# Four layers on one core: the first pair's layer norm in the last spectral round spread over every second product, its roots made together, and the first projections one product later

## The chip, the core and the metric

The program runs on one core of a Trainium2 chip as a single launch. The metric is the device time of one execution in microseconds (us); three executions of the kernel before gave a median of 2034.66 us (2031.99 to 2038.42). A core has a matrix engine (PE), a vector engine (DVE), an activation engine (ACT), a general engine (POOL) and a queue for transfers (SP). Each runs its instructions in the order in which they stand in its own queue; an instruction that waits for another engine holds up all that stand behind it.

## The reference

The input x has 2048 rows of 640 values. Four layers follow each other, each with a norm ahead and a residual sum behind: spectral, attention, spectral, attention.

```
def layernorm(x): return (x - mean(x)) / sqrt(var(x) + 1e-5)          # over the 640 columns

def spectral(x):                       # real part of a two-dimensional Fourier transform
    a, b = x @ Wd_re.T, x @ Wd_im.T
    return Ws_re @ a - Ws_im @ b

def attention(x):                      # 32 heads of 20, each query sees 256 keys back
    q, k, v = split(x @ wqkv)
    return softmax(mask(q @ k.T * 20 ** -0.5)) @ v @ wo

x = x + spectral(layernorm(x));  x = x + attention(layernorm(x))      # twice over
```

## The kernel before

Rows go in 16 tiles of 128. A number in f32 that enters a matrix product is split in two halves of 16 bits, a high one (rounded by ACT) and a low one (the rest, made by DVE or POOL), and a product is made of three: high by high, high by low, low by high.

**A spectral layer** has four rounds (`r`), each over four tiles of the transformed input, and in each round eight steps (`j`), each for two tiles of 128 output rows. A step makes seven products of twelve matmuls (128x320). `main_a` makes one (`x`), `main_c` then closes the step before with two (`z`, `y`), `main_b` makes four (`y`, `x`, `z`, `y`); so a row of products reads x z y | y x z y. The letters are banks of the matrix memory (PSUM). Three products of a step start a bank and are later added to in place: the second half of such a pair may not begin until the add that reads the first half is done (DVE, `add`, L583, written `res<-z`, `res<-y`, `pf<-y`). After the last round the sums are the next layer's input, written to DRAM (`x2d`).

Beside its products a step prepares the seven factors of the step after. A block of the matrix comes by DMA (`cq`, 1 MB), POOL makes four sums of its quarters (`cs`, L549 to L552), ACT makes seven high halves (`cc`, L557), DVE seven low halves (`cc`, L560). Input blocks, sums, and later the stacked keys share three large buffers, so one is filled when the last reader of what was there is done.

**What sets the order.** Behind each product stands a call of `tick()`. It lets out the next split (one low half and the next high half) and takes one step of every generator in the list `side`; a generator's `yield` thus means "go on after the next product". A scheduler then sets each engine's own order from this; it keeps dependencies and such marks as `issue_after`, and can let an instruction pass others of its engine. The order rows in the prediction are what stands in each queue in the end.

**The last round** (`r == NR - 1`) prepares the attention as well. When step 0 is closed, its two output tiles are the first pair of rows for the attention. `finish(j, pace)` (L655) loads them back, takes the steps of `norm_steps` with `pace` yields for each, then transposes the two normed tiles on PE (`transposed`, L449: a block of three and one of two 128x128 transposes for each tile, `pf<-idf,lny`; ACT copies the high half, L455, DVE takes the low one, L456). The side list holds `finish(0, 1)` for the first pair and behind it, in one chain, `finish(1, 1)` for the second. `ahead` (L643), put on the list at step 3, waits until the first pair is transposed, yields once, and then makes ten projection products of 15 matmuls each (`Projections.qk`, L370, 128x256), five for the keys and five for the queries of the first block, one per tick. ACT takes each out of PSUM (`qf`, L386), POOL splits it (L387, L388), SP stores it (`qkd<-early`). At the head of step 7 whatever `ahead` has left is run at once, and the stacks of keys and queries are loaded (`ks<-onesd`, `ks<-qkd`). Behind the last product `drain()` runs what the side list still holds, and the attention begins with a value projection (`pf<-big,early`, 15 matmuls 128x320, taken out by ACT L902) and scores (`sq<-ks`). Transposes, projections and value projections all take their PSUM bank from one ring of two (`new_f`).

**`norm_steps`** (L131) first takes two `bn_stats` halves and a `bn_aggr` for each tile (L138, L141; a yield after the first half and one after the sum), then the inverse root by bits and three Newton steps on columns of one value per row: for each tile L147, L148, three times L150 and L151, and with `act` L155; two yields per tile. With `act`, two more yields and then one ACT pass per tile (L163, `lny`). For a pair this is 4 + 4 + 2 + 2 = 12 yields. `finish` is the only caller with a pair and `act`.

The last round occurs twice, once in each spectral layer; its steps 3 to 7 lie at about 464 to 548 us and 1470 to 1554 us of the profile.

Of the kernel before, what the change touches and what calls it, by code (L numbers as in the profile page):

```python
# [13 lines left out]
I32 = mybir.dt.int32  # L14
AF = mybir.ActivationFunctionType
OP = mybir.AluOpType
# [38 lines left out]
ROOT = float(0x5F3759DF - (1 << 22) - (1 << 30))  # L55
# [9 lines left out]
X_UP = 2.0 ** 10  # L65
# [8 lines left out]
def body(ctx: ExitStack, tc: tile.TileContext, x_in, cmat, whid, wqkv, wo, out):  # L74
    nc = tc.nc
# [40 lines left out]
    normed = [None]  # L116
# [14 lines left out]
    def norm_steps(xs, ys, act=False):  # L131

        n = len(xs)
        mv = keep.tile([P, n, 2], F32, tag=f"lnmv{n}", name="lnmv", bufs=2)
        for k, x in enumerate(xs):
            st = keep.tile([P, 2, 6], F32, tag="lnst", name="lnst", bufs=2)
            for h in range(2):
                nc.vector.bn_stats(st[:, h], x[:, h * 320:(h + 1) * 320])  # L138
                if h == 0:
                    yield  # L140
            nc.vector.bn_aggr(mv[:, k], st.rearrange("p a b -> p (a b)"))  # L141
            yield
        t = keep.tile([P, 3, n], F32, tag=f"lnt{n}", name="lnt", bufs=2)
        ts = nc.vector.tensor_scalar
        for k in range(n):
            h, g, u = (t[:, m, k:k + 1] for m in range(3))
            ts(h, mv[:, k, 1:2], 1e-5, -0.5 * X_UP ** -2, op0=OP.add, op1=OP.mult)  # L147
            ts(g.bitcast(I32), h.bitcast(I32), -0.5, ROOT, op0=OP.mult, op1=OP.add)  # L148
            for m in range(3):
                ts(u, g, g, h, op0=OP.mult, op1=OP.mult)  # L150
                normed[0] = ts(g, u, 1.5, g, op0=OP.add, op1=OP.mult).ins  # L151
                if m == 0:
                    yield
            if act:
                normed[0] = ts(u, mv[:, k, 0:1], g, -1.0, op0=OP.mult, op1=OP.mult).ins  # L155
            yield
        for _ in range(2 if act else 0):
            yield
        for k, x in enumerate(xs):
            g, u = t[:, 1, k:k + 1], t[:, 2, k:k + 1]  # L160
            y = keep.tile([P, D], F32, tag="lny", name="lny", bufs=2)
            if act:
                nc.scalar.activation(y, x, AF.Identity, bias=u, scale=g)  # L163
            else:
                normed[0] = ts(y, x, mv[:, k, 0:1], g, op0=OP.subtract, op1=OP.mult).ins
            ys.append(y)
            yield

    def layer_norm(xs):
        ys = []  # L170
        for _ in norm_steps(xs, ys):
            pass
        return ys
# [7 lines left out]
    def load(out, in_):  # L181
        with ExitStack() as order:
            if in_turn[0] and loads:
                order.enter_context(tc.issue_after(loads[-1]))
            elif floor:
                order.enter_context(tc.issue_after(floor[-1]))
            i = nc.sync.dma_start(out, in_)
        loads.append(i.ins)
# [211 lines left out]
    def spectral(layer, res_src, hidden, first):  # L400
        with ExitStack() as st:
# [11 lines left out]
            splits, side, marks = [], [], {}  # L413
# [8 lines left out]
            def tick(cut=True):  # L422
                if splits and cut:
                    with behind():
                        for f in splits.pop(0):
                            f()
                with behind():
                    for g in list(side):
                        if next(g, None) is None:
                            side.remove(g)  # L430
# [18 lines left out]
            def transposed(y, k, xt):  # L449
                d0, d1 = ((0, 3), (3, ND))[k]  # L450
                pt = new_f()[:, :(d1 - d0) * P].rearrange("p (a b) -> p a b", a=d1 - d0)
                for dt in range(d0, d1):
                    transpose(pt[:, dt - d0], y[:, dt * P:(dt + 1) * P], idf)
                hi, lo = (xt[:, m, d0:d1] for m in range(2))
                nc.scalar.activation(hi, pt, AF.Copy)  # L455
                nc.vector.scalar_tensor_tensor(lo, pt, 1.0, hi, op0=OP.mult, op1=OP.subtract)  # L456
# [50 lines left out]
            def side_norm(s):  # L507
                x, ys = load_x(s), []
                for _ in range(3):
                    yield 1  # L510
                for _ in norm_steps([x], ys, True):
                    yield 1
                split_x(s, ys[0], nc.gpsimd)
                yield 1
# [55 lines left out]
            def product(r, bank, cc, m, start, stop):  # L570
                o = bank[:, :HD]
                n = 0
                for k in range(RS):
                    zc = hidden.zc[RS * r + k]
                    for a, b in ((0, 0), (0, 1), (1, 0)):
                        matmul(o, cc[m][:, a, k * P:(k + 1) * P], zc[:, m, b],
                                         start=start and n == 0, stop=stop and n == 3 * RS - 1,
                                         skip_group_check=True)
                        n += 1
                return o  # L580

            def add(o, z, f):
                marks["dve"] = nc.vector.scalar_tensor_tensor(o, z, Y_DOWN, f, op0=OP.mult, op1=OP.add).ins  # L583
# [44 lines left out]
            def main_c(r, j):  # L628
                res, cc, y, zb = state.pop((r, j))
                x0, x1 = res  # L630
                z = product(r, zb, cc, 6, False, True)
                add(x0[:, hi], z, x0[:, hi])
                tick()
                z = product(r, y, cc, 5, False, True)
                add(x1[:, lo], z, x1[:, lo])
                last = r == NR - 1
                for k in range(2):
                    load((x2_d if last else acc_d)[2 * j + k], res[k])
                if last and j == 0:
                    side.append(chain(finish(0, 1), finish(1, 1)))  # L640
                tick()

            def ahead(proj):  # L643
                while finished[0] < 2:
                    yield 1
                yield 1
                for w in (1, 0):
                    for ct in range(ND):
                        for _ in proj.qk(0, w, ct):
                            pass  # L650
                        yield 1
# [3 lines left out]
            def finish(j, pace):  # L655
                xs = [sb.tile([P, D], F32, tag="xin", name="x2", bufs=NXIN) for k in range(2)]
                for k in range(2):
                    load(xs[k], x2_d[2 * j + k])
                for _ in range(3):
                    yield 1  # L660
                ys = []
                for _ in norm_steps(xs, ys, True):
                    for _ in range(pace):
                        yield 1
                for _ in range(2):
                    yield 1
                proj.new_rows(j)
                for k, y in enumerate(ys):
                    for m in range(2):
                        transposed(y, m, proj.rows[j][0][:, k])  # L670
                        yield 1
                    finished[0] += 1
# [95 lines left out]
            for r in range(NR):  # L768
# [24 lines left out]
                for j in range(NJ):  # L793
                    n = r * NJ + j
# [5 lines left out]
                    if r == NR - 1 and j == 3:  # L800
                        early_qk = ahead(proj)
                        side.append(early_qk)
# [20 lines left out]
                    with ExitStack() as order:  # L823
                        if j == 0 and r == 0 and first:
                            order.enter_context(tc.issue_after(hidden.last))
                        main_a(r, j)
                        if j:
                            main_c(r, j - 1)
                        main_b(r, j)
                    if r < NR - 1 and j in STAGES[r]:  # L830
                        k = STAGES[r].index(j)
                        s = RS * (r + 1) + k
                        turned_x(s)
                        if k < RS - 1:
                            turn_x(s + 1, 2)
                        z_stage(s)
                main_c(r, NJ - 1)
                if r == NR - 1:
                    drain()
# [672 lines left out]
```

## Time and profile before

| | |
|---|---|
| three executions, median (range) | 2034.66 us (2031.99 to 2038.42) |
| the profiled execution | 2034.73 us |
| its span, first to last instruction | 2033.0 us |
| PE busy | 1978.8 us, 97% |
| DVE busy | 1556.2 us, 77% |
| POOL busy | 1438.2 us, 71% |
| ACT busy | 1098.1 us, 54% |
| mean granted PE clock | 0.999 |

The profile is of one execution. A row of a timeline reads: start and length in us, engine, line, operation, what it writes and reads, shapes, and a count where like instructions follow each other; in square brackets the time that the engine stood idle before it and what ended the wait. Lengths of matmuls overlap: a row's next start less its start is what it costs PE. Line numbers are those of the kernel before.

### The profile page before, as it was taken

What the parts mean: (1) busy time and instruction counts of PE and PEld (TensorE: products, weight loads), DVE (VectorE), ACT (ScalarE), POOL (GpSimd) and SP (SyncE); (2) the same over time, 40 slices, a digit from 0 to 9 for tenths busy, and PEclk for the clock granted to TensorE, in tenths of its full rate; (3) what the DMA queues carried; (4) which work ended last, traced back from release to release, by engine and by line L of the source; (5) the groups of instructions that cost most, each with busy time, mean ns of one, the idle gap of its engine ahead of it and who ended that gap; (6) DMA issues with size and microseconds to landing.
All of it is one profiled execution on the core that took longest, in us unless ns stands there. A gap on an engine that the chain in (4) does not pass through costs nothing.

```text
span 2033.0 us, 55567 instructions
## 1 busy us (share of the span) xinstructions
PE 1978.8 (97%) x21761; PEld 1446.6 (71%) x21761; DVE 1556.2 (77%) x3281; ACT 1098.1 (54%) x1962; POOL 1438.2 (71%) x2148
## 2 busy tenths in 40 slices
PE   7999999999999999999999999999999999999998
PEld 5777777776777777777667777777677677777765
DVE  8888788767688888777648778787766788886674
ACT  5444555543257677666644444444332577766665
POOL 4667788877568788765557778777774687777754
PEclk9999999999999999999999999999999999999999
DMA  8566467566545545434545465454754455443232
GB/s 276 185 195 212 167 212 233 184 240 213 144 99 130 126 112 122 101 100 114 157 133 179 157 183 183 150 171 150 266 184 122 106 124 123 118 120 94 75 81 80
DMA packets 280507, 311.08 MB, mean 153 GB/s; under 512 B 107572, under 2 KB 214836, under 8 KB 271156
## 3 DMA queue, kind: packets, MB, share of 16 engines
q1 hardware_dynamic: 279668, 306.88, 51.3%
q8 instruction: 170, 2.79, 0.6%
q14 instruction: 93, 0.76, 0.1%
q10 hardware_dynamic: 576, 0.66, 0.1%
HBM read 201.72 MB, written 83.46 MB: 140 GB/s over the span
## 4 chain that ended last, share of the span: by engine, by line
PE 72%; DVE 12%; issue 4%; ACT 3%; DMA 2%; POOL 2%; SPq 0%; DVEq 0%; ACTq 0%; POOLq 0%
PE pf L125 33%; PE y L125 12%; PE x L125 12%; PE z L125 8%; PE sk L125 5%; DVE cc L560 3%; PE sq L125 3%; DVE sq L1216 2%; ACT ptq L1272 2%; DVE m L1218 2%; DMA res<-accd 1%; DVE lnst L138 1%; DVE lnt L150 1%; DVE res L583 1%; DVE lnt L151 1%
## 5 line engine op out<-in xcount | busy, mean ns | idle before, releaser
L125 PEld LDWEIGHTS <-cc 128*128 128x128 f16 x5376 | 525.9, 98 | 211.2 <-issue 11.1
L1272 ACT ACTIVATE ptq<-sk,shift,alpha 128x768 f32<-128x768 f32 (+2 forms) x512 | 472.7, 945 | 134.2 <-PE sk L125 70.5
L125 PEld LDWEIGHTS <-big 128*128 128x128 f16 x4320 | 411.9, 98 | 132.9 <-issue 27.0
L1218 DVE TENSOR_REDUCE m<-sq 128x2 f32<-128x512 f32 (+1 forms) x512 | 345.2, 674 | 18.9
L557 ACT ACTIVATE cc<-cs 128x512 f16<-128x512 f32 x256 | 153.1, 623 | 273.0 <-POOL cs L550 151.5
L125 PE MATMUL pf<-early,big 128*128 128x256 f16 x2400 | 288.1, 273 | 4.2 <-ACT qf L386 3.8
L1216 DVE COPY_PREDICATED sq<-mask,sk 128x256 f32<-128x256 int32 x512 | 216.4, 423 | 69.3 <-PE sq L125 65.9
L125 PE MATMUL y<-zc,cc 128*128 128x320 f16 x1728 | 262.1, 299 | 3.2 <-DVE pf L583 3.2
L1276 POOL TENSOR_SCALAR_AFFINE_SELECT ptq<-ptq 128x512 f32<-128x512 f32 x224 | 142.7, 637 | 170.6 <-ACT ptq L1272 169.2
L560 DVE SCALAR_TENSOR_TENSOR cc<-cs,cc 128x512 f16<-128x512 f32 x256 | 246.4, 971 | 6.0 <-ACT cc L557 6.0
L560 DVE SCALAR_TENSOR_TENSOR cc<-cq,cc 128x512 f16<-128x512 f32 x192 | 204.4, 1066 | 0.1
L125 PE MATMUL pf<-ptq,v 128*32 128x128 f32 (+1 forms) x3840 | 183.9, 330 | 4.8 <-DVE x L990 3.7
L125 PE MATMUL z<-zc,cc 128*128 128x320 f16 x1152 | 177.7, 299 | 2.9 <-DVE res L583 1.9
L1278 POOL TENSOR_SCALAR_AFFINE_SELECT ptq<-ptq 128x512 f32<-128x512 f32 x256 | 164.6, 643 | 22.4 <-ACT ptq L1272 22.3
L125 PE MATMUL x<-zc,cc 128*128 128x320 f16 x1152 | 177.7, 299 | 0.0
L549 POOL TENSOR_TENSOR cs<-cq 128x512 f32<-128x512 f32 x64 | 85.3, 1333 | 87.8 <-DVE cc L560 64.8
L386 ACT ACTIVATE qf<-pf 128x256 f32<-128x256 f32 x160 | 60.9, 382 | 156.4 <-PE pf L125 108.4
L125 PEld LDWEIGHTS pf<-ptq,v 128*32 128x32 f32 x3840 | 110.9, 110 | 47.5 <-DVE x L990 5.7
L125 PE MATMUL pf<-big,early 128*128 128x320 f16 x960 | 141.4, 300 | 0.0
L125 PEld LDWEIGHTS <-qs 62*128 62x128 f16 x2688 | 90.2, 94 | 59.2 <-issue 56.0
L279 POOL TENSOR_TENSOR zc<-big,zc 128x320 f16<-128x320 f32 x96 | 74.7, 792 | 73.6 <-ACT zc L278 73.6
L125 PE MATMUL pf<-bo,ot 128*128 128x320 f16 x840 | 124.6, 301 | 0.8 <-DVE x L990 0.8
(147 smaller groups left out, 3443.3 us busy)
## 6 DMA issues: line engine op xcount, KB each, us to landing
cq<-in_cmat_dram SPq DMA_DIRECT2D x64, 1024.0 KB
accd<-res SPq DMA_DIRECT2D x96, 320.0 KB
res<-accd SPq DMA_DIRECT2D x96, 320.0 KB
x<-x2d SPq DMA_DIRECT2D x64, 320.0 KB
qkd<-early SPq DMA_DIRECT2D x160, 128.0 KB
ks<-qkd SPq DMA_DIRECT2D x108, 160.0 KB
qs<-qkd SPq DMA_DIRECT2D x84, 160.0 KB
x2d<-res SPq DMA_DIRECT2D x32, 320.0 KB
```

Source lines behind the costliest of these rows:

```text
L125: i = getattr(nc.tensor, what)(*args, **kw)
L138: nc.vector.bn_stats(st[:, h], x[:, h * 320:(h + 1) * 320])
L279: nc.gpsimd.tensor_tensor(zc[:, m, 1], f, zc[:, m, 0], op=OP.subtract)
L386: nc.scalar.activation(f, pf[:, :QB], AF.Copy, scale=down)
L549: g.tensor_tensor(s1, a21, a22, op=OP.add)
L557: nc.scalar.activation(cc[m][:, 0], f, AF.Copy, scale=C_UP)
L560: nc.vector.scalar_tensor_tensor(cc[m][:, 1], f, C_UP, cc[m][:, 0], op0=OP.mult, op1=OP.subtract)
L1216: marks["dve"] = nc.vector.copy_predicated(near[pi][:, :, 0], mask[:, None, :].to_broadcast([P, 2, P]), farq[pi]).ins
L1218: marks["dve"] = nc.vector.tensor_reduce(TOP[n][:, pi, :, k], near[pi][:, :, :1 + (i >= 1)], axis=AX.XY, op=OP.max).ins
L1272: marks["act"] = nc.scalar.activation(o[:, pi], tps[pi][:, :, first:], AF.Sigmoid, bias=shift, scale=alpha[:, 0:1]).ins
L1276: nc.gpsimd.affine_select(out=q[:, :, a0], in_=q[:, :, a0], pattern=[[0, 4], [-1, P]], base=0, channel_multiplier=1, compare_op=OP.is_gt, ...
L1278: ins = nc.gpsimd.affine_select(out=q[:, :, a0 + 2], in_=q[:, :, a0 + 2], pattern=[[0, 4], [1, P]], base=0, channel_multiplier=-1, compare ...
```

## The change

It has three parts.

- `norm_steps` for a pair with `act` no longer goes tile by tile. The root columns of both tiles are worked on together, on 128x2 operands, and the pointer forms become tensor operations: a start of two instructions, three Newton steps of three (two `tensor_tensor`, one `scalar_tensor_tensor`) with a yield after each, and one instruction for the bias. That is 12 small instructions instead of 18, and 3 + 1 yields where there were 4: 12 in all, as before.
- `finish(0, 1)` becomes `finish(0, 2)`: each of the 12 yields of the first pair's norm is taken twice.
- `ahead` yields twice, not once, after the first pair is transposed.

The second pair keeps its pace of one, and has the new roots as well. Lines of the kernel after stand 11 later from L145 of before on, and 12 later from L647 on.

```
--- before.py
+++ after.py
@@ -142,7 +142,18 @@
         t = keep.tile([P, 3, n], F32, tag=f"lnt{n}", name="lnt", bufs=2)
         ts = nc.vector.tensor_scalar
-        for k in range(n):
+        if n > 1 and act:
+            h, g, u = (t[:, m] for m in range(3))
+            ts(h, mv[:, :, 1], 1e-5, -0.5 * X_UP ** -2, op0=OP.add, op1=OP.mult)
+            ts(g.bitcast(I32), h.bitcast(I32), -0.5, ROOT, op0=OP.mult, op1=OP.add)
+            for m in range(3):
+                nc.vector.tensor_tensor(u, g, g, op=OP.mult)
+                nc.vector.tensor_tensor(u, u, h, op=OP.mult)
+                normed[0] = nc.vector.scalar_tensor_tensor(g, u, 1.5, g, op0=OP.add, op1=OP.mult).ins
+                yield
+            normed[0] = nc.vector.scalar_tensor_tensor(u, mv[:, :, 0], -1.0, g, op0=OP.mult, op1=OP.mult).ins
+            yield
+        for k in range(0 if n > 1 and act else n):
             h, g, u = (t[:, m, k:k + 1] for m in range(3))
@@ -637,13 +648,14 @@
                 if last and j == 0:
-                    side.append(chain(finish(0, 1), finish(1, 1)))
+                    side.append(chain(finish(0, 2), finish(1, 1)))
                 tick()
 
             def ahead(proj):
                 while finished[0] < 2:
                     yield 1
-                yield 1
+                for _ in range(2):
+                    yield 1
                 for w in (1, 0):
```

## The prediction

> **What bounds the kernel now.** I read the page first (PE busy 97% of the span), then the stretches, then PE's timeline in the last round of the first spectral layer, PE's waits at the same place of the second, and last the queues that PE waits for. Columns of the stretch: PE, PEld, DVE, ACT and POOL busy, granted clock, DMA share, GB/s.
>
> ```profile
> 460.00:485.00 25.00, 22.36 (x166) 16.01 (x164) 24.72 (x54) 11.66 (x22) 18.74 (x14) 1.00 0.70 243
> ```
>
> ```profile
> 466.93 1.79 PE L125 MATMUL z<-zc,cc 128*128 128x320 f16 x12 [1.05 <-DVE res L583]
> 470.32 3.42 PE L125 MATMUL y<-zc,cc 128*128 128x320 f16 x24 [1.59 <-DVE pf L583]
> ...
> 494.39 1.80 PE L125 MATMUL pf<-early,big 128*128 128x256 f16 x15 [1.47 <-ACT qf L386]
> ```
>
> ```profile
> PE y L125 <- DVE pf L583: 1.6, 1, 1.6
> PE pf L125 <- ACT qf L386: 1.5, 1, 1.5
> PE z L125 <- ACT cc L557: 1.0, 1, 1.0
> ```
>
> The kernel is bound by PE at full clock. In this round PE waits three times, 1.05 + 1.59 + 1.47 = 4.11 us, and the same three times in the second layer (last fence; the releaser of the third differs, the sizes don't). So 8.2 us, 0.40% of 2034.73, is all that the change can remove here. The first two waits come from DVE, which is full in that stretch (24.72 of 25.00 us): `z` and `y` are second halves of pairs, and wait for the add that reads the first half. 0.3% (6.1 us) is about what a measurement of this kernel can tell from no change.
>
> **Part 1, the first pair's norm.** DVE's rows ahead of those two adds:
>
> ```profile
> 465.23 0.19 DVE L141 BATCH_NORM_AGGREGATE lnmv<-lnst 128x2 f32<-128x12 f32 x1
> ...
> 465.36 0.87 DVE L560 SCALAR_TENSOR_TENSOR cc<-cq,cc 128x512 f16<-128x512 f32 x1
> 466.16 0.26 DVE L150 TENSOR_SCALAR lnt<-lnt 128x1 f32<-128x1 f32 x1
> ...
> 466.40 0.47 DVE L583 SCALAR_TENSOR_TENSOR res<-z,res 128x320 f32<-128x320 f32 x1
> 466.80 0.20 DVE L151 TENSOR_SCALAR lnt<-lnt 128x1 f32<-128x1 f32 x1
> ...
> 466.98 1.35 DVE L560 SCALAR_TENSOR_TENSOR cc<-cs,cc 128x512 f16<-128x512 f32 x1
> 468.25 0.44 DVE L150 TENSOR_SCALAR lnt<-lnt 128x1 f32<-128x1 f32 x2
> ...
> 469.78 0.48 DVE L583 SCALAR_TENSOR_TENSOR pf<-y,pf 128x320 f32<-128x320 f32 x1
> ...
> 478.43 0.48 DVE L583 SCALAR_TENSOR_TENSOR res<-z,res 128x320 f32<-128x320 f32 x1
> ```
>
> DVE's order at this place before (the second tile's second `bn_stats`, then the roots among adds and splits):
>
> ```order
> L138 BN_STATS lnst<-x_5631 128x6
> L147 TENSOR_SCALAR lnt<-lnmv 128x1
> L583 SCALAR_TENSOR_TENSOR res<-x,res 128x320
> L141 BN_AGGR lnmv<-lnst 128x2
> L148 TENSOR_SCALAR lnt<-lnt 128x1
> L560 SCALAR_TENSOR_TENSOR cc<-cq,cc 128x512
> L150 TENSOR_SCALAR lnt<-lnt 128x1
> L147 TENSOR_SCALAR lnt<-lnmv 128x1
> L583 SCALAR_TENSOR_TENSOR res<-z,res 128x320
> ```
>
> and now (L594 is the add, L571 the split):
>
> ```order
> L594 SCALAR_TENSOR_TENSOR res<-x,res 128x320
> L571 SCALAR_TENSOR_TENSOR cc<-cq,cc 128x512
> L138 BN_STATS lnst<-x_5631 128x6
> L594 SCALAR_TENSOR_TENSOR res<-z,res 128x320
> L141 BN_AGGR lnmv<-lnst 128x2
> L571 SCALAR_TENSOR_TENSOR cc<-cs,cc 128x512
> L594 SCALAR_TENSOR_TENSOR pf<-y,pf 128x320
> L571 SCALAR_TENSOR_TENSOR cc<-cs,cc 128x512
> L147 TENSOR_SCALAR lnt<-lnmv 128x2
> L571 SCALAR_TENSOR_TENSOR cc<-cs,cc 128x512
> L148 TENSOR_SCALAR lnt<-lnt 128x2
> L150 TENSOR_TENSOR lnt<-lnt 128x2
> ```
>
> All four `bn_stats` still stand ahead of the read of `z`; only root steps moved behind `pf<-y`. So `res<-z` comes 0.13 (465.23 to 465.36) + 0.24 (466.16 to 466.40) = 0.37 earlier, and PE's first wait shrinks to 0.68. `pf<-y` loses another 0.18 (466.80 to 466.98) and 1.53 (468.25 to 469.78) and has the 0.12 of the sum in front: 1.96 earlier, 467.82, read by 468.30. PE would be there at 470.32 - 1.59 - 0.37 = 468.36: the second wait is gone.
>
> But the roots come back. PE reaches its next accumulating `z` six products later, at 468.36 + 6 x 1.63 = 478.14. DVE's read of that bank stood at 478.43; it moves by -1.96, by -0.25 for two old root steps, and by three new groups: 0.13 + 0.19 for the start and three instructions each time, which no row shows in this form. Their nearest rows:
>
> ```profile
> 509.03 0.27 DVE L150 TENSOR_SCALAR lnt<-lnt 128x1 f32<-128x1 f32 x1
> 509.34 0.21 DVE L151 TENSOR_SCALAR lnt<-lnt 128x1 f32<-128x1 f32 x1
> ```
>
> I take 0.21 each, 0.65 per group; 0.31 (dependent starts) is the high end. 478.43 - 2.21 + 0.32 + 1.95 = 478.49, read by 478.97, so PE waits 0.9 anew. Before, 1.2 us of transposes stood on PE in this stretch and gave DVE that time; they move away. Net gain 2.64 - 0.68 - 0.90 = **1.06 us a layer**; 0.2 if each small instruction costs 0.31, 1.96 if the new roots hide.
>
> **Part 2, the projections.** Yields: the first pair takes 3 + 24 + 2 + 4 = 33 ticks (21 before). There are 40 from its start to the head of step 7 and 49 to the last product. So `ahead` starts 13 ticks later; the order has four projections among the products of step 6 and six in a row at the head of step 7. What stopped PE at 494.39 before:
>
> ```profile
> 480.94 0.33 SPq L187 DMA_DIRECT2D cq<-in_cmat_dram  x1
> 481.37 0.38 SPq L187 DMA_DIRECT2D res<-accd  x1
> ```
>
> ```profile
> 486.92 1.31 POOL L603 TENSOR_TENSOR res<-res,pf 128x320 f32<-128x320 f32 x1 [3.91 <-DVE pf L583]
> ```
>
> ```profile
> 489.49 0.63 ACT L557 ACTIVATE cc<-cs 128x512 f16<-128x512 f32 x1 [5.95 <-POOL cs L549]
> ...
> 493.97 0.64 ACT L386 ACTIVATE qf<-pf 128x256 f32<-128x256 f32 x2
> ```
>
> `qf` stood on ACT behind the splits of `cs`, whose sums POOL began late, behind an add whose loaded tile (`res`, I take it) had been queued on SP behind `cq`. Now that load stands ahead of `cq`, and ACT's order at the projections is this, first before, then now (L568 is the split, L397 `qf`, L613 the copy of a step's first product):
>
> ```order
> L557 ACTIVATE cc<-cs 128x512 x3
> L557 ACTIVATE cc<-cq 128x512
> L386 ACTIVATE qf<-pf 128x256 x4
> L602 ACTIVATE pf<-x 128x320
> L557 ACTIVATE cc<-cs 128x512
> ```
>
> ```order
> L613 ACTIVATE pf<-x 128x320
> L568 ACTIVATE cc<-cs 128x512
> L568 ACTIVATE cc<-cq 128x512 x2
> L568 ACTIVATE cc<-cs 128x512 x3
> L397 ACTIVATE qf<-pf 128x256 x10
> ```
>
> The ten copies stand together, behind splits whose sums were made a step earlier. I take the whole **1.47 us a layer** as gone (0 if the splits are late again). The burst of six costs PE nothing: a product is 1.63, POOL's two steps on it 0.45 + 0.78, the `qf` copies 0.39 or less.
>
> ```profile
> L388 POOL TENSOR_TENSOR early<-qf,early 128x256 f16<-128x256 f32 x10 | 7.8, 780 | 0.7
> ...
> L387 POOL CAST early<-qf 128x256 f16<-128x256 f32 x10 | 4.5, 446 | 1.3 <-ACT qf L386 1.3
> ```
>
> **Part 3, the second pair falls off the end.** 33 + 21 = 54 ticks, and there are 49: its four transpose blocks run in `drain()`, behind the last product. ACT's order there, before and now:
>
> ```order
> L455 ACTIVATE early<-pf 128x384
> L455 ACTIVATE early<-pf 128x256
> L1411 ACT_TABLE_LOAD
> L1411 ACTIVATE first<-shift 128x1
> L902 ACTIVATE v<-pf 128x16x20 x2
> ```
>
> ```order
> L1423 ACT_TABLE_LOAD
> L1423 ACTIVATE first<-shift 128x1
> L466 ACTIVATE early<-pf 128x384
> L466 ACTIVATE early<-pf 128x256
> L466 ACTIVATE early<-pf 128x384
> L466 ACTIVATE early<-pf 128x256
> L914 ACTIVATE v<-pf 128x16x20 x2
> ```
>
> The copies now stand behind the table load, and nothing on PE covers them.
>
> ```profile
> 530.30 0.49 PE L125 MATMUL pf<-idf,lny 128*128 128x128 f32 x3
> 530.63 1.79 PE L125 MATMUL y<-zc,cc 128*128 128x320 f16 x12
> ...
> 547.69 2.20 PE L125 MATMUL pf<-big,early 128*128 128x320 f16 x15
> 549.83 0.28 PE L125 MATMUL sq<-ks 62*128 62x128 f16 x4
> ```
>
> ```profile
> 530.83 0.49 ACT L455 ACTIVATE early<-pf 128x384 f16<-128x384 f32 x1 [3.30 <-PE pf L125]
> ...
> 547.96 1.28 ACT L1411 ACT_TABLE_LOAD   x1 [11.09 <-PE y L125]
> 549.25 0.20 ACT L1411 ACTIVATE first<-shift 128x1 f32<-128x1 f32 x1
> ```
>
> ```profile
> 1553.88 0.20 ACT L1411 ACTIVATE first<-shift 128x1 f32<-128x1 f32 x1 [11.11 <-PE y L125]
> ```
>
> ```profile
> 535.74 0.56 DVE L456 SCALAR_TENSOR_TENSOR early<-pf,early 128x384 f16<-128x384 f32 x1 [0.85 <-ACT early L455]
> ...
> 548.51 0.55 DVE L859 MEMSET sk<- 128x256 f32 x2
> ```
>
> Blocks and the value projection share two banks: block 3 waits for block 1's low half, the projection for block 3's. Count from the end of PE's last product (547.69 before, when the projection began at once). Second layer: block 1 at 0; ACT at 0.53 (530.30 to 530.83), done 1.02; DVE, behind a memset until 1.10, done 1.65; block 3 at 1.70; ACT 2.23 to 2.72; DVE 2.76 to 3.31; projection at 3.37. First layer: the table load waits for PE's last product (0.27 to 1.55), `first` to 1.76, ACT 1.76 to 2.25, DVE 2.85, block 3 at 2.90, then as above: 4.56. The ten transposes no longer stand among the products: 0.33 for three, 1.10 in all. **Cost 2.27 + 3.46 = 5.73 us**; 4.5 if the chain runs bare in both layers (2 x 1.68 - 1.10 each), 7.7 if DVE's memset and second low half each time come ahead.
>
> By the Trainium skill (ScalarE: Activation LUTs, section What ACT_TABLE_LOAD costs) a switch is a load of about 1283 ns and a drain of about 1380 ns. The row has the load, and `first` starts 0.01 us behind it, so no such drain follows here; with one the first layer's tail would be 5.94 and the sum 1.38 higher.
>
> **Sum.** 5.73 - 2 x 1.06 - 2 x 1.47 = +0.67 on 2034.73, 2035.4 for an execution like the profiled one; that lies 0.07 above the median, so 2035.3. Ends: 4.5 - 3.92 - 2.94 = -2.4 and 7.7 - 0.4 = +7.3.
>
> **The rivals.**
>
> *The stacks come late (slower).* The last projection ends nine products, 14.7 us, before PE's last product, no longer 31 us.
>
> ```profile
> 537.17 6.31 SPq L187 DMA_DIRECT2D ks<-qkd  x6
> ```
>
> From its end: 2.2 until its store is issued, four key loads at 1.05, six query loads at 6.31: issued by 12.7. The scores come at 14.7 + 3.37 + 2.14 = 20.2. Before, the last load was issued at 543.48 and the scores at 549.83 did not wait, so landing takes under 6.35: 19.1. It decides from 1.1 us more on. If SP needs 15 us where I count 10.5 the scores wait 3.4: +6.8 + 0.7, 2042.2. Chance 0.12.
>
> *The waits for DVE only move.* DVE is full, the new roots are as slow as the old, and part 1 gains nothing: 5.73 - 2.94 = +2.8, 2037.5. Chance 0.17.
>
> *PE runs cold behind the tail (slower).* At half clock the 2.14 of the value projection double: +4.3 + 0.7, 2039.7, and more if the scores are cold too.
>
> ```profile
> 0.00:8.40 8.40, 0.00 (x0) 0.00 (x0) 4.49 (x22) 2.72 (x3) 1.27 (x11) 1.00 0.78 266
> 8.40:10.00 1.60, 1.37 (x6) 1.00 (x7) 1.60 (x4) 1.40 (x4) 0.00 (x0) 1.00 0.98 315
> ```
>
> Against it: behind 8.40 us without a matmul the granted clock reads 1.00, and the longest hole of the tail would be 2.25 us (0.65 to 2.90). The Trainium skill (TensorE: Matmul & The Clock Gate, section What's actually happening) lets an idle window of about 3.4 us halve the clock; no run here shows it. Chance 0.03.
>
> *Everything hides (faster).* All 8.2 us go and the tail costs PE one chain instead of two (1.68 - 1.10 a layer): -7.1, 2027.6. The order speaks against it: the projection's bank is block 3's. Chance 0.04.
>
> **The numbers.** Forecast 0.64, gains and tail cancel. 2030.5 to 2041.5: the ends above less what the three runs scatter below, and up to where the late stacks begin. Faster by over 0.3% 0.05, within 0.81, slower 0.14.
>
> **What would show it.** After: the waits at `y` and at `qf` gone, a shorter one at `z`, a new one of about 0.9 two steps on; PE idle 2 and 1 us around the transposes behind the last product, longer in the first layer; the table load ahead of the copies. Wrong if scores wait for `ks<-qkd`, if the projections wait in the burst, or if PE's holes at the end are under 1.5 or over 5 us.

## The result, and where the time went

The kernel after takes 2047.11 us (median of four executions, 2045.97 to 2048.18) against 2034.08 for the kernel before (four executions, 2031.99 to 2038.42): ratio 1.0062, 95% interval 1.005 to 1.0075. The forecast was 2035.3, 2030.5 to 2041.5; the kernel is slower, and by more than the range allowed. The profiled execution of the kernel after took 2046.32 us. Its page begins:

```profile
span 2044.5 us, 55549 instructions
...
PE 1980.2 (97%) x21761; PEld 1444.8 (71%) x21761; DVE 1563.5 (76%) x3257; ACT 1099.0 (54%) x1962; POOL 1437.2 (70%) x2148
```

Nothing stands out there: the span is 11.5 us longer than before, and PE's busy time by 1.4. So nearly all of it is waiting, and it has to be looked for in the round that was changed. I measure this round from the moment PE stops at the first accumulating `z` (its start less its wait) to the first value projection: before 547.69 - (466.93 - 1.05) = 81.81 us in the first layer and 81.79 in the second, after 88.89 and 86.08. That is 7.08 + 4.29 = 11.37 of the 11.5. (Outside the round, the start of the first one lies 2.23 us later, the stretch between the two is 1.54 shorter and what follows 0.56 shorter, which nearly cancels. The rounds are read from one execution of each kernel, here and below.) PE's waits from 455 to 560 us (us in total, times, longest), and the rows of PE's timeline behind them:

```profile
PE pf L125 <- DVE early L467: 5.1, 3, 2.1
PE z L125 <- DVE res L594: 2.8, 3, 1.2
PE y L125 <- DVE pf L594: 1.7, 1, 1.7
```

```profile
469.29 1.79 PE L125 MATMUL z<-zc,cc 128*128 128x320 f16 x12 [1.18 <-DVE res L594]
...
479.34 1.79 PE L125 MATMUL y<-zc,cc 128*128 128x320 f16 x12 [1.67 <-DVE pf L594]
...
483.81 1.79 PE L125 MATMUL z<-zc,cc 128*128 128x320 f16 x12 [1.05 <-DVE res L594]
...
500.11 0.49 PE L125 MATMUL pf<-idf,lny 128*128 128x128 f32 x3
...
506.14 0.55 PE L125 MATMUL pf<-idf,lny 128*128 128x128 f32 x3 [2.06 <-DVE early L467]
...
528.01 9.99 PE L125 MATMUL pf<-early,big 128*128 128x256 f16 x90
...
552.50 0.71 PE L125 MATMUL pf<-idf,lny 128*128 128x128 f32 x5
555.29 0.77 PE L125 MATMUL pf<-idf,lny 128*128 128x128 f32 x5 [2.08 <-DVE early L467]
557.00 2.20 PE L125 MATMUL pf<-big,early 128*128 128x320 f16 x15 [0.95 <-DVE early L467]
```

Read against the forecast. The wait for `qf` is gone and the burst of six projections (`x90`) runs without a gap, as forecast. The tail, from the first block behind the last product (552.50) to the value projection (557.00), is 4.50 where 4.56 was forecast; in the second layer 1562.27 to 1565.66, 3.39 where 3.37 was. The waits for DVE in the round (the third at `z`, 0.55 at 457.76, lies ahead of it), though, are 1.18 + 1.67 + 1.05 = 3.90 where 2.64 stood before and 1.58 was forecast. And one wait was on no list: the third transpose block of the first pair waits 2.06.

**DVE.** Its rows from the first wait to the root steps, and POOL's rows of the same time:

```profile
466.99 1.45 DVE L571 SCALAR_TENSOR_TENSOR cc<-cq,cc 128x512 f16<-128x512 f32 x1
...
468.77 0.47 DVE L594 SCALAR_TENSOR_TENSOR res<-z,res 128x320 f32<-128x320 f32 x1
...
471.46 0.82 DVE L147 TENSOR_SCALAR lnt<-lnmv 128x2 f32<-128x2 f32 x1
...
473.18 0.16 DVE L151 TENSOR_TENSOR lnt<-lnt 128x2 f32<-128x2 f32 x1
...
474.64 1.26 DVE L151 TENSOR_TENSOR lnt<-lnt 128x2 f32<-128x2 f32 x1
475.94 1.19 DVE L152 SCALAR_TENSOR_TENSOR lnt<-lnt 128x2 f32<-128x2 f32 x1
...
480.49 0.82 DVE L150 TENSOR_TENSOR lnt<-lnt 128x2 f32<-128x2 f32 x1
481.34 0.79 DVE L151 TENSOR_TENSOR lnt<-lnt 128x2 f32<-128x2 f32 x1
```

```profile
466.62 1.27 POOL L563 TENSOR_TENSOR cs<-cq,cs 128x512 f32<-128x512 f32 x1
467.85 1.32 POOL L624 TENSOR_TENSOR res<-res,pf 128x320 f32<-128x320 f32 x1
...
471.02 1.24 POOL L635 TENSOR_TENSOR res<-res,pf 128x320 f32<-128x320 f32 x1 [1.03 <-DVE pf L594]
474.62 1.27 POOL L560 TENSOR_TENSOR cs<-cq 128x512 f32<-128x512 f32 x1 [2.36 <-DVE lnt L150]
475.85 1.27 POOL L562 TENSOR_TENSOR cs<-cq 128x512 f32<-128x512 f32 x1
...
479.98 1.31 POOL L614 TENSOR_TENSOR res<-res,pf 128x320 f32<-128x320 f32 x1
481.25 0.86 POOL L624 TENSOR_TENSOR res<-res,pf 128x320 f32<-128x320 f32 x1
```

The same instruction (L151) takes 0.16 at 473.18 and 1.26 at 474.64. Each long root row ends when a POOL operation that was under way ends: 471.46 + 0.82 = 472.28 against 471.02 + 1.24 = 472.26, 474.64 + 1.26 = 475.90 against 475.89, and so on. Against 0.16 each, the five lose 4.1 us of a full DVE. The add of 468.77 is not held: it also has two tensors, but one of them (`z`) is in PSUM, and it takes 0.47 although POOL is at work from 467.85 to 469.17.

**The third block.** ACT's rows, and the POOL row that they wait for:

```profile
503.45 1.15 ACT L568 ACTIVATE cc<-cs 128x512 f16<-128x512 f32 x2 [2.72 <-POOL cs L561]
504.51 0.61 ACT L568 ACTIVATE cc<-cq 128x512 f16<-128x512 f32 x1
505.03 0.74 ACT L466 ACTIVATE early<-pf 128x384 f16<-128x384 f32 x2
```

```profile
501.70 1.72 POOL L561 TENSOR_TENSOR cs<-cs,cq 128x512 f32<-128x512 f32 x1
```

The copies of the first two blocks (L466) stand on ACT behind splits whose sum POOL ends at 503.42. Block one was on PE at 500.11; its copy comes 4.9 us later, its low half (L467) behind that, and block three needs the bank.

**The clock.** Stretches right behind this wait (PE, PEld, DVE, ACT, POOL busy, granted clock, DMA share, GB/s), and the same place in the second layer:

```profile
506.14:507.00 0.86, 0.86 (x7) 0.73 (x8) 0.86 (x2) 0.28 (x1) 0.00 (x0) 1.00 0.00 0
507.00:508.00 1.00, 1.00 (x6) 0.58 (x5) 1.00 (x4) 0.21 (x1) 0.69 (x1) 0.56 0.07 16
508.00:509.00 1.00, 1.00 (x6) 0.58 (x4) 1.00 (x1) 0.00 (x0) 1.00 (x2) 0.50 0.00 0
509.00:510.00 1.00, 1.00 (x6) 0.77 (x5) 1.00 (x4) 0.19 (x1) 1.00 (x1) 0.50 0.00 0
510.00:511.00 1.00, 1.00 (x8) 0.60 (x6) 1.00 (x2) 0.19 (x1) 1.00 (x2) 0.73 0.00 0
```

```profile
1517.59:1519.00 1.41, 1.41 (x11) 1.13 (x12) 1.41 (x4) 0.49 (x1) 0.24 (x1) 1.00 0.00 0
```

In the first layer PE ran at half clock for 0.88 + 1 + 1 + 0.54 = 3.42 us (each stretch's distance from 1.00 over 0.50), which costs half of that, 1.7 us. The second layer had the same wait and no loss of clock. This is why the first layer lost 2.8 us more than the second: 1.7 here, 1.1 in the longer tail.

### The profile page after: what moved, and what is told of

Same layout as the page of the kernel before. It is cut to its first block, busy times and chain, and to the rows that moved or that the text cites. A ratio compares the mean times of both kernels' runs of the same rounds, so it can differ in the third digit from the quotient of the medians.

```text
span 2044.5 us, 55549 instructions
## 1 busy us (share of the span) xinstructions
PE 1980.2 (97%) x21761; PEld 1444.8 (71%) x21761; DVE 1563.5 (76%) x3257; ACT 1099.0 (54%) x1962; POOL 1437.2 (70%) x2148
## 4 chain that ended last, share of the span: by engine, by line
PE 67%; DVE 14%; issue 4%; DMA 3%; ACT 3%; POOL 2%; SPq 0%; DVEq 0%; ACTq 0%; POOLq 0%
PE pf L125 32%; PE x L125 10%; PE y L125 10%; PE z L125 7%; PE sk L125 5%; DVE cc L571 4%; PE sq L125 3%; DVE sq L1228 2%; ACT ptq L1284 2%; DVE m L1230 2%; DMA res<-accd 1%; DVE res L594 1%; DVE lnst L138 1%; DVE lnt L161 1%; DMA xin<-in_x_dram 1%
## 5 line engine op out<-in xcount | busy, mean ns | idle before, releaser
L571 DVE SCALAR_TENSOR_TENSOR cc<-cq,cc 128x512 f16<-128x512 f32 x192 | 209.7, 1093 | 0.1
```

What stands on the lines that cost most here:

```text
L571: nc.vector.scalar_tensor_tensor(cc[m][:, 1], f, C_UP, cc[m][:, 0], op0=OP.mult, op1=OP.subtract)
```

## The experiments

The theories. **A**: the new root instructions are held while a POOL operation runs; the 128x1 instructions before were not. **B**: it is the pace that puts too much between the adds. **C**: it is the bunching of a pair's root steps. **T**: the tail costs what was forecast. **H**: the third block waits because its neighbours' copies stand behind late splits at this product. **Q**: the wait at the third projection went with the order of SP's queue. **W**, formed later: a form is held if its row has an even count of values side by side.

The table has each kernel's median, its ratio to runs of the kernel before on the same chip (95% interval; their medians were 2035.65, 2035.07 and 2035.46 in the three groups of runs behind the first comparison), and the round in both layers, measured as above in the profiled execution.

| kernel | us | ratio | round, us |
|---|---|---|---|
| before | 2034.08 | 1 | 81.81, 81.79 |
| after | 2047.11 | 1.0062 (1.0050 to 1.0075) | 88.89, 86.08 |
| old roots, paced | 2042.38 | 1.0036 (1.0022 to 1.0049) | 85.38, 84.28 |
| pointer forms | 2043.66 | 1.0039 (1.0027 to 1.0052) | 85.44, 84.33 |
| three columns | 2046.14 | 1.0051 (1.0038 to 1.0063) | 87.26, 87.81 |
| joint roots alone | 2031.93 | 0.9982 (0.9974 to 0.9991) | 79.91, 79.91 |
| later projections alone | 2030.10 | 0.9978 (0.9970 to 0.9987) | 80.17, 80.17 |
| both, no pace | 2031.22 | 0.9979 (0.9970 to 0.9987) | 79.91, 79.92 |
| joint roots, transposes later | 2031.20 | 0.9979 (0.9970 to 0.9988) | 80.39, 80.39 |
| second pair apart | 2040.07 | 1.0021 (1.0013 to 1.0030) | 85.28, 83.81 |
| apart, transposes later | 2033.69 | 0.9999 (0.9990 to 1.0008) | 81.55, 81.54 |
| apart, later, pointer forms | 2027.92 | 0.9968 (0.9956 to 0.9980) | 78.75, 78.96 |

**Old roots, paced.** The new block of `norm_steps` is taken out of the kernel after.

```
-        if n > 1 and act:
...
-        for k in range(0 if n > 1 and act else n):
+        for k in range(n):
```

> The kernel after with the old roots (128x1, tile by tile, four yields each) but the pace of two and the later projections kept. Theory A (the 128x2 root instructions are held while a POOL operation runs): the root instructions cost 0.12 to 0.28 again, PE's waits for DVE in steps 3 to 5 fall from 3.90 us a layer to under 2, the wait at the third transpose block (2.06) and the tail (4.50 and 3.39) stay; about 2042.5, ratio 1.004. Theory B (spreading the norm itself puts too much on DVE between the adds): the waits stay at 3.9 a layer and the time at about 2047, ratio 1.006.

The waits for DVE are 1.18 + 0.22 = 1.40 a layer in place of 3.90, and the time is 2042.4: A, and not B. The first of them stays at 1.18, since all root steps come behind it. The wait at the third block grew to 2.88, since PE now arrives earlier at copies that come no sooner.

**Pointer forms.** The roots of the kernel after, grouped as there, in 128x1 instructions (the Newton steps are shown; start and bias are changed alike).

```
...
-                nc.vector.tensor_tensor(u, g, g, op=OP.mult)
-                nc.vector.tensor_tensor(u, u, h, op=OP.mult)
-                normed[0] = nc.vector.scalar_tensor_tensor(g, u, 1.5, g, op0=OP.add, op1=OP.mult).ins
+                for h, g, u in c:
+                    ts(u, g, g, h, op0=OP.mult, op1=OP.mult)
+                for h, g, u in c:
+                    normed[0] = ts(g, u, 1.5, g, op0=OP.add, op1=OP.mult).ins
...
```

> The kernel after, its roots in the same four groups and at the same products, but each group made of 128x1 instructions with pointer operands (18, not 12). Theory A: only the form counts, so PE's waits for DVE fall by 2 us a layer or more, about 2042.5, ratio 1.004. Theory C (it is the bunching of a pair's root steps at one product that holds up the adds, not the form): more instructions in the same bunches, waits of 3.9 a layer or more, 2047 or above.

1.19 + 0.27 = 1.46 a layer: more instructions in the same bunches, and the waits go. Not C; the form counts.

**Joint roots alone**, in the kernel before.

> The kernel before with the joint roots alone; pace one and the projections where they were. Theory A: the twelve 128x2 instructions lose some 4 us of DVE a layer and pair, PE's waits for DVE (2.64 a layer) grow by 1 to 4; 2036 to 2042, slower than before. Theory B: twelve small instructions in place of eighteen, waits the same or shorter; 2032 to 2035.

Here A's expectation failed: the kernel is faster than before, and no wait of `z` or `y` for DVE is left in the round (a wait of 1.53 at `z` for ACT's split, and 0.92 at the third block, take their place). DVE and POOL of this kernel show why; first two of DVE's root rows, then POOL's row:

```profile
470.43 0.82 DVE L152 SCALAR_TENSOR_TENSOR lnt<-lnt 128x2 f32<-128x2 f32 x1
...
471.77 0.15 DVE L150 TENSOR_TENSOR lnt<-lnt 128x2 f32<-128x2 f32 x1
```

```profile
474.04 1.27 POOL L560 TENSOR_TENSOR cs<-cq 128x512 f32<-128x512 f32 x1 [2.81 <-DVE cc L571]
```

Of the twelve, three are held (0.82, 0.51, 0.82); the last seven, from 471.77 to 473.36, fall into POOL's idle 2.81 us and take 0.15 or 0.16 each. The forms are not slow in themselves: at a pace of one nine of twelve met an idle POOL, at a pace of two five of twelve met a busy one, and those stood at the adds that PE waits for.

**The forms by themselves.** A small program runs each form twelve times with POOL idle, then beside POOL's additions.

> Not the kernel: the output is a copy of the input, and DVE runs nine kinds of instruction twelve times each, first with POOL idle, then with POOL running 150 128x320 additions one behind the other. Theory A: alone every small kind takes 0.1 to 0.3 us; beside POOL the forms that stood long in the kernel after (tensor_tensor, scalar_tensor_tensor and immediate tensor_scalar on 128x2) take 0.6 to 1.3, the 128x1 pointer forms stay under 0.3, and the 128x512 scalar_tensor_tensor goes from 0.68 to 1.2 or more. Rival: the long instructions of the kernel after came from something else (a dependence, a semaphore), and all small forms stay under 0.4 beside POOL.

One row for each form (ns: min/median/max): `scalar_tensor_tensor` 128x2, immediate `tensor_scalar` 128x2, pointer `tensor_scalar` 128x1, first alone, then beside POOL; last the 128x2 `tensor_scalar` with two pointers.

```profile
L40 DVE SCALAR_TENSOR_TENSOR v<-v x12: 154/161/163, 32.0 to 34.1; 128x2 f32<-128x2 f32 x12
L42 DVE TENSOR_SCALAR v<-v x12: 168/169/171, 34.3 to 36.6; 128x2 f32<-128x2 f32 x12
L46 DVE TENSOR_SCALAR v<-v x12: 272/274/274, 39.0 to 42.4; 128x1 f32<-128x1 f32 x12
```

```profile
L40 DVE SCALAR_TENSOR_TENSOR v<-v x12: 778/779/809, 77.2 to 86.2; 128x2 f32<-128x2 f32 x12
L42 DVE TENSOR_SCALAR v<-v x12: 778/779/786, 87.0 to 96.0; 128x2 f32<-128x2 f32 x12
L46 DVE TENSOR_SCALAR v<-v x12: 272/272/274, 99.0 to 102.4; 128x1 f32<-128x1 f32 x12
L50 DVE TENSOR_SCALAR v<-v x12: 286/288/73969, 105.7 to 183.0; 128x2 f32<-128x2 f32 x12
```

A is shown: 0.16 becomes 0.78 beside a POOL addition of 0.86, and the pointer form on one column doesn't change. The kernel's split form, 128x512, went from 0.75 to 1.42. The last row is one instruction that was held for 73.97 us, till POOL's additions were over, some 87 of them (73.97 / 0.85).

**Other widths**, in the same small program, and **three columns** in the kernel after (a third, unused column beside the pair's two).

```
+        wide = 3 if n > 1 and act else n
...
-        t = keep.tile([P, 3, n], F32, tag=f"lnt{n}", name="lnt", bufs=2)
+        t = keep.tile([P, 3, wide], F32, tag=f"lnt{wide}", name="lnt", bufs=2)
```

> Not the kernel: DVE alone, then beside POOL's 150 additions, with the forms at other widths: tensor_tensor and scalar_tensor_tensor on 128x1, both and the immediate tensor_scalar on 128x3, the three on 128x2 with every second column, and scalar_tensor_tensor on 128x2 as before. Theory W (a form is held when its row has an even count of values that lie side by side): 128x1, 128x3 and the spread 128x2 stay at 0.15 to 0.2 beside POOL, only the last goes to 0.78. Rival (a form is held when it has over one value in a row, or two tensors): 128x3 and the spread ones go to 0.78 too.

> The kernel after, with a third, unused column beside the two of the pair, so that its joint root instructions are 128x3 at the same places (one small memset more for each pair). Theory W: none is held, PE's waits for DVE in steps 3 to 5 fall from 3.90 us a layer to about 1.46 as with the pointer forms, 2042 to 2043.7. Rival: held as at 128x2, the waits stay at 3.9 and the time at 2047.

Beside POOL, `scalar_tensor_tensor` on 128x1 and immediate `tensor_scalar` on 128x3:

```profile
L42 DVE SCALAR_TENSOR_TENSOR v<-v x11: 778/782/782, 54.3 to 62.5; 128x1 f32<-128x1 f32 x11
```

```profile
L45 DVE TENSOR_SCALAR v<-v x12: 780/781/790, 82.8 to 91.8; 128x3 f32<-128x3 f32 x12
```

W falls: 128x1 with two tensors, 128x3 and every second column are all held at 0.78, and with three columns the kernel waits 1.21 + 1.67 + 1.05, as the kernel after does with two. What stays free in the runs is `tensor_scalar` on one column, with immediates or with pointers: just the form that the change replaced. The Trainium skill (SBUF — State Buffer, section Who interferes with whom) says that a DVE instruction with two inputs in SBUF contends with a POOL instruction that reads SBUF, and it calls the port pair that the two engines share an exclusive lock. The runs agree (0.16 against 0.78). It names `tensor_scalar` as one that can contend too; in the runs it does on two and three columns, and not on one.

**Second pair apart.** It is taken out of the chain and begins behind step 4.

```
-                    side.append(chain(finish(0, 2), finish(1, 1)))
+                    side.append(finish(0, 2))
+                if last and j == 4:
+                    side.append(finish(1, 1))
```

> The kernel after, but the second pair's norm begins behind step 4 by itself, five products earlier than the chain lets it, so that its transposes come before the last product. Theory T (the tail costs 4.50 + 3.39 and the transposes among the products 1.10 a layer): no PE wait between the last product and the value projection, 5.7 us less than after, 2041.4, ratio 1.0035. Rival: the second pair's blocks now meet the burst of projections in the ring of two banks, or its held roots the adds, and give 2 us a layer or more back: 2045 or above.

The tail is gone, and the round is 3.61 and 2.27 us shorter than after; forecast for the tail were 3.46 and 2.27. T holds. The first layer again had half clock behind its 2.05 us at the third block, the second not.

**Apart, transposes later.** The first pair's blocks come two products later.

```
-                for _ in range(2):
+                for _ in range(4 if pace > 1 else 2):
                     yield 1
                 proj.new_rows(j)
```

> The kernel with the second pair apart, and the first pair's transposes two products later. Theory H (the third block waited 2.06 because the copy of the first block stands on ACT behind splits of late sums, at this product and no other; the half clock of the first layer follows from that hole): no wait of over 0.5 at the transposes, no stretch under a clock of 0.9, 4.1 us less for the holes and 1.5 for the clock than with the second pair apart alone: about 2035 where that had 2040. Rival: the copies are late wherever the blocks stand, as ACT is behind by as much at every product: 2039 to 2041.

No wait at the blocks, no half clock in the round, 3.73 and 2.27 us less than with the second pair apart alone; what is left is the three waits for DVE, 3.92 us. H holds here.

**Joint roots, transposes later**, by one product, in the kernel before with the joint roots.

> The kernel before with the joint roots, and the first pair's transposes one product later. Theory H: the wait of 0.92 a layer at the third block goes, 1.8 us less than with the joint roots alone, which had 2031.9: about 2030. Rival: PE then waits as long for the next factor's high half, since ACT and POOL are what it has caught up with: 2031.5 to 2032.5.

H's expectation failed: the wait at the third block went from 0.92 to 1.39. DVE's low half of the first block (L467, at 483.30) stood behind an add that itself waited 0.76 us for POOL. So a block's place has to suit ACT and DVE both; one product later suited ACT alone. The time hardly moved (2031.2 against 2031.9).

**Later projections alone**, the third part of the change, in the kernel before.

> The kernel before with the projections one product later and nothing else. Theory Q (the wait of 1.47 a layer at the third projection goes with the order of SP's queue and the sums of POOL, which here stay as they were): the wait stays, moved to another projection, 2034 to 2036. Rival (one product's delay is enough for the copies to come behind the splits): the wait goes, 2.9 us less than before, 2032.5.

The wait goes, so Q is not the whole of it: 1.63 us of delay is more than the 1.47 that the third projection waited. The round gains 1.64 and 1.62; the median gained 5.0, of which the round explains 3.3, and the rest I can't place. **Both, no pace**:

> The kernel before with the joint roots and the projections one product later, the pace of one kept: the kernel after without its pace. If the two parts add up (each alone took away 1.6 to 1.9 us a layer of the round, the wait at the projections in both): about 2030, waits of 1.5 at z for ACT's split and 0.9 at the third block, none at the end. If the loss of the kernel after comes from the later projections beside the joint roots: 2035 or more.

Both together gain no more than the roots alone (79.91). The joint roots had removed that wait too, with the projections where they were: there the load of `res` is issued at 476.75, ahead of `cq` at 480.38, as the forecast had it for the kernel after. One wait can be removed only once.

**All three repairs.**

> The kernel after with all three repairs: pointer forms in the roots, the second pair apart, the first pair's transposes two products later. If the three causes are separate, the round costs 81.55 - 2.45 = 79.1 us a layer, against 81.8 before: 2.7 less a layer, about 2029.5. If the transposes then meet a busy DVE again, as when they were moved by one product beside the joint roots: 2 us a layer more, 2033.

PE's waits in the round of the first layer are two:

```profile
467.06 1.79 PE L125 MATMUL z<-zc,cc 128*128 128x320 f16 x12 [0.74 <-DVE res L598]
480.60 3.42 PE L125 MATMUL y<-zc,cc 128*128 128x320 f16 x24 [0.27 <-DVE pf L598]
```

2027.92 us, ratio 0.9968 (0.9956 to 0.9980): faster than both kernels, with the pace, the bunches and the later projections all kept.

## Why the prediction was wrong

The forecast was +0.67 for the profiled execution; 11.59 came. In the round of both layers:

- **Part 3, the tail: right.** Forecast 5.73; the kernel after less the one with the second pair apart is 3.61 + 2.27 = 5.88. The table load ahead of the copies, `first` 0.01 us behind it and the shared banks came as worked out.
- **Part 2, `qf`: right in size.** The wait went, and the burst cost nothing. The reason given for it is not shown: with the later projections alone the load of `res` stays behind `cq`, and the wait goes as well.
- **Parts 1 and 2 together** were forecast at 2 x (1.06 + 1.47) = 5.06 of gain. With pointer forms and without tail and third-block wait the gain is 163.60 - 157.71 = 5.89. With the 128x2 forms at the same places it is 163.60 - 163.09 = 0.51. **The step that failed is the price in part 1**: "I take 0.21 each, 0.65 per group; 0.31 (dependent starts) is the high end". The nearest rows were of another form, one that POOL did not hold in any run here, and the true high end was a whole POOL operation, 1.26. So the bound was too narrow, and "+7.3" with it. The row that told was in the forecast: the 128x512 split, also of two tensors, stood there at 0.87 and at 1.35. I read past the difference. The held roots delayed first the `y` at 479.34 (1.67), ahead of the `z` at which the forecast expected 0.9 and where 1.05 came. The first wait was mis-sized too, whatever the form of the roots (1.18 with the old ones): the split ahead of `res<-z` took 0.87 before and 1.45 after (it stood beside the POOL operation of 466.62 to 467.89), and 1.18 was left where 0.68 was forecast.
- **The third block: not foreseen.** Moving the first pair's blocks was priced only by the 1.2 us of PE time that DVE no longer gets, not by what stands on ACT ahead of their copies at the new place. Between the kernels with and without it lie 3.73 + 2.27 = 6.00, of which 4.1 is the wait and 1.7 the clock.
- -0.51 + 6.00 + 5.88 = 11.37, which is the round's loss. Of the miss, 4.55 lies in parts 1 and 2, where the 128x2 forms cost 163.09 - 157.71 = 5.38 and the rest came out 0.83 better than forecast; 6.00 is the third block, 0.15 the tail.

Of the rivals, the late stacks did not come (no wait for `ks` in the round). "The waits for DVE only move" came, at a higher price. The cold PE came too: in this execution behind the third block and not behind the tail, for 3.4 us. That the tail was spared here was luck. The kernels with the old roots and with three columns have the same tail, and in their profiled executions the half clock fell on the first layer's value projection (3.87 and 3.77 us where it takes 2.20 here):

```profile
551.82 3.87 PE L125 MATMUL pf<-big,early 128*128 128x320 f16 x15 [0.95 <-DVE early L456]
```

The chance of 0.03 was set by the hole of 8.40 us at the start; the same profile had a stretch at 0.50 behind a wait of 1.81 us (below), which the forecast did not look at.

The range's lower end does not come out of its own words (2034.66 - 2.4 - 2.67 = 2029.6, where 2030.5 stands); nothing hangs on it here.

## What to carry to other kernels

Price an instruction by a row of the same form, and look at what POOL does at its new place: two tensors in SBUF, or several columns, on DVE may wait for a whole POOL operation (a second tensor in PSUM did not), and eighteen small pointer instructions can be cheaper than twelve wide ones. When a step moves, look up on every engine that handles its output what stands ahead of it there. A part that gains alone (the joint roots, 0.9982) can lose in company, so parts are to be run apart.

## What the runs showed of the hardware

**Half clock behind short holes.** In the twelve traces of the whole kernel I looked for every PE wait of 1.3 us or more behind the start-up, and every stretch of 3 us with a clock under 0.93. There are 28 waits of 1.8 to 2.9 us, and behind 12 of them, all between 1.81 and 2.08, comes a stretch of half clock; behind waits of 1.3 to 1.7 there is none, nor behind the four of 2.87 to 2.90. In the kernel before it was this one, in the attention, PE's row and two stretches behind it:

```profile
1000.13 0.31 PE L125 MATMUL sk<-ks,qs 62*128 62x128 f16 x4 [1.81 <-ACT ptq L1272]
```

```profile
1002.00:1003.00 1.00, 1.00 (x20) 0.68 (x15) 0.97 (x3) 0.82 (x1) 0.11 (x1) 0.50 0.83 315
1003.00:1004.00 1.00, 1.00 (x14) 0.40 (x7) 0.56 (x1) 0.18 (x1) 1.00 (x2) 0.50 0.83 131
```

So a wait of about 2 us carries a risk of some 1.7 us more, here in 12 of the 24 cases of 1.81 to 2.08. What decides was not tried. The Trainium skill (TensorE: Matmul & The Clock Gate, section What's actually happening) tells of a window of 3413 ns that runs free of the kernel; a stretch of 3.42 us and the same wait with and without a loss would fit that, but the waits here are shorter than the idle window that it names.
